# Hedgehog attention with layer norm and MLP: centring as a one-input operation, the layer norm weight moved into the PSUM copies and into w1

## The chip, the cores and the metric

The kernel runs on one core of a Trainium2 chip. The metric is the device time of one execution in microseconds. A core has a TensorE (PE, with weight loads as a second stream, PEld), a VectorE (DVE), a ScalarE (ACT), a GpSimd (POOL), and SyncE (SP), which issues most of the DMAs. All executions quoted here are fast ones by the label that each result carries. Where two kernels are compared, the ratio is the mean time of one kernel's fast runs over the mean of the other's fast runs of the same rounds, with a 95% interval. It is therefore not quite the ratio of the medians quoted beside it.

## The reference

Eight batches, eight heads, 576 positions, head size 64, 128 features. The attention's result is the input of a layer norm and a two-layer MLP with a residual.

```python
def _attn_ref(q, k, v, w_phi):
    def phi(x):
        proj = np.einsum('bhsd,df->bhsf', x, w_phi)
        proj = proj - np.max(np.abs(proj), axis=-1, keepdims=True)
        return np.concatenate([np.exp(proj), np.exp(-proj)], axis=-1)
    q_p, k_p = (phi(q), phi(k))
    kv = np.einsum('bhsf,bhsd->bhfd', k_p, v)
    z = np.sum(k_p, axis=2)
    num = np.einsum('bhsf,bhfd->bhsd', q_p, kv)
    den = np.einsum('bhsf,bhf->bhs', q_p, z)[..., None] + 1e-06
    return num / den

def _moe_ref(x, g_ln, w_ch1, w_ch2):          # x: 8 x 576 x 512
    mu = np.mean(x, axis=-1, keepdims=True)
    var = np.mean((x - mu) ** 2, axis=-1, keepdims=True)
    xn = (x - mu) / np.sqrt(var + 1e-06) * g_ln
    ch = np.maximum(xn @ w_ch1, 0.0) @ w_ch2  # 512 -> 2048 -> 512
    return x + ch
```

Dividing by the standard deviation commutes with the rectifier and with both products, so the kernel applies it at the very end. Only (x − mean)·g has to be ready ahead of the first product. The weight g belongs to a column of x, that is, to a row of w_ch1. So it can be multiplied into x, into the transposed x, or into w_ch1.

## The kernel before

The work goes in four pairs of batches. Each pair has nine tiles of 128 rows, taken in three rounds. For each tile, DVE makes the statistics, one engine centres (tile `xc`), the rows are transposed (`xT`; for pair 0 by the TensorE through PSUM, for the other pairs by a transposing DMA), and the products `hT_ps` (w1) and `ch_ps` (w2) follow. While the MLP of one pair runs, the attention of the next one is woven in between.

The order on each engine is not written by hand. Every operation is handed to a list scheduler with its inputs, its outputs and a **told duration for each engine that could do it**. `add_any` lets the scheduler choose the engine. Told durations steer the order; they are not what the chip takes. A change of one told number can therefore reorder everything behind it.

```python
            def center(e, i=i, t=t):
                ...
                if e == "DVE":
                    nc.vector.scalar_tensor_tensor(
                        out=xc, in0=x[:, t, :], scalar=pr["mv"][:, t, 0:1],
                        in1=gln_sb, op0=ALU.subtract, op1=ALU.mult,
                    )
                else:
                    xd = moe_sb.tile([P, DM], FP32, tag="xd", name="xd", bufs=1)
                    nc.gpsimd.tensor_tensor(
                        out=xd, in0=x[:, t, :], in1=bcast(pr["mv"][:, t, 0], 1, DM),
                        op=ALU.subtract,
                    )
                    nc.gpsimd.tensor_tensor(out=xc, in0=xd, in1=gln_sb, op=ALU.mult)
            ...
            add("DVE", 0.72, V, stats, ...)
            add_any({"DVE": 0.62, "POOL": 2.1}, V, center, ...)
...
            def copy(e, k0=k0, st=st):                      # pair 0 only: PSUM -> xT
                copy_on(
                    e, pr["xT", r][:, k0 : k0 + 2, 0:cols],
                    st["ps"][:, 0 : 2 * cols].rearrange("p (k n) -> p k n", k=2),
                )
            add_any({"DVE": 0.08 + 0.128 * n, "ACT": 0.12 + 0.21 * n}, V, copy, ...)
...
    dma("SP", 3.0, 262144, gln_sb, dram(moe_g_ln, 0, [[0, P], [1, DM]]), w=["gln"])
...
    FAST, SLOW, MOE_STEP = 4.9, 10.5, 0.92                  # spacing of the MLP's ranks
```

## Time and profile before

| | before |
|---|---|
| median of the three runs ahead of the prediction | 380.05 us (378.9 to 380.62) |
| profiled run: span, mean granted TensorE clock | 378.5 us, 0.982 |
| matmuls | 3348 |
| centrings | 19 on DVE, 17 on GpSimd (two operations each) |

The prediction below shows the page's busy shares and slices, windows of 10 us, a timeline and the groups. Two more windows of the kernel before are needed for the comparison. They come from the view that sums the busy time of each engine in a stretch; the columns are: stretch, length, then busy us and instruction count of PE, PEld, DVE, ACT, POOL, then the granted clock, the DMA share and GB/s.

```profile
80.00:100.00 20.00, 19.41 (x240) 12.30 (x239) 18.89 (x51) 17.85 (x49) 17.75 (x31) 1.00 0.86 182
120.00:140.00 20.00, 20.00 (x194) 11.65 (x193) 14.52 (x44) 11.32 (x28) 12.99 (x20) 1.00 0.73 185
```

The TensorE has next to no holes in either stretch. In the first, DVE has 1.1 us to spare in 20, in the second 5.5 us.

And from the view of waits of the TensorE, between 60 and 145 us (who waits for whom: total us, times, longest), all that it lists:

```profile
PE xT_ps L938 <- POOL xc L891: 0.5, 1, 0.5
PE pm L572 <- ACT ea L676: 0.3, 1, 0.3
PE kv L696 <- POOL vv L646: 0.2, 1, 0.2
```

### The profile page before, as it was taken

The page shows a single profiled execution, that of the slowest core. Times are in us where ns is not written, and L with a number is a line of the kernel's source. Part 1 is how long each engine was busy: PE and PEld are TensorE (multiplying, and loading weights), DVE is VectorE, ACT ScalarE, POOL GpSimd, SP SyncE. Part 2 cuts the span into 40 slices and gives each one's busy share as a digit, 9 for nine tenths or more (in the row PEclk, how much of TensorE's full clock was granted, in tenths as well). Part 3 has the DMA queues.
Part 4 walks back from the last instruction along what each step waited for, and adds up shares of the span by engine and source line. Part 5 has one row for each costly group of instructions (what it writes and reads, how often), then busy time and mean ns, then how long its engine had stood idle before and what let it go on. Part 6 is the DMA issues. An engine that isn't in the chain of part 4 may idle for free.

```text
span 378.5 us, 9097 instructions
## 1 busy us (share of the span) xinstructions
PE 351.5 (93%) x3348; PEld 207.8 (55%) x3348; DVE 275.4 (73%) x723; ACT 251.8 (67%) x640; POOL 207.3 (55%) x368
## 2 busy tenths in 40 slices
PE   3786589999999999999999999999999999999995
PEld 1464367556566555655556555555565545555553
DVE  3889989799879768977879999976767885000102
ACT  3999489799879638876689556977779306433310
POOL 5589669889857658864456647953546432000000
PEclk9999579999999999999999999999999999999999
DMA  6999999998949834488555743712200135110102
GB/s 177 282 264 228 174 281 258 272 165 142 280 138 238 237 100 99 83 182 226 172 134 141 223 99 78 174 29 58 58 28 29 50 88 102 28 57 28 55 32 83
DMA packets 88749, 52.70 MB, mean 139 GB/s; under 512 B 55040, under 2 KB 84096, under 8 KB 88704
## 3 DMA queue, kind: packets, MB, share of 16 engines
q1 hardware_dynamic: 83856, 47.37, 49.5%
q0 software_dynamic: 4224, 4.19, 6.8%
q10 hardware_dynamic: 624, 0.56, 0.5%
q8 instruction: 26, 0.43, 0.4%
q14 instruction: 19, 0.16, 0.2%
HBM read 37.03 MB, written 9.44 MB: 123 GB/s over the span
## 4 chain that ended last, share of the span: by engine, by line
PE 65%; ACT 5%; DVE 4%; POOL 2%; issue 1%; DVEq 0%; POOLq 0%; DMA 0%
PE ch_ps L1021 27%; PE hT_ps L989 27%; PE num L730 3%; PE kv L701 3%; ACT ea L676 2%; PE pm L572 2%; ACT EB L623 2%; DVE m L592 1%; PE pt L670 1%; DVE st L873 1%; ACT hT L999 1%; PE kv L696 1%; POOL xc L891 1%; POOL xd L887 1%; DVE xc L881 1%
## 5 line engine op out<-in xcount | busy, mean ns | idle before, releaser
L989 PE MATMUL hT_ps<-xT,w 128*128 128x384 bf16 x768 | 150.2, 327 | 1.0 <-ACT EB L623 0.7
L1021 PE MATMUL ch_ps<-w,hT 128*128 128x512 bf16 (+2 forms) x592 | 148.5, 373 | 0.0
L999 ACT ACTIVATE hT<-hT_ps 128x384 bf16<-128x384 f32 x130 | 63.9, 502 | 62.1 <-PE hT_ps L989 61.8
L989 PEld LDWEIGHTS <-w 128*128 128x128 bf16 x768 | 71.4, 98 | 54.4 <-issue 4.1
L592 DVE TENSOR_REDUCE m<-pm 128x4 f32<-128x512 f32 x128 | 82.1, 678 | 7.9 <-PE pm L572 7.5
L754 POOL TENSOR_TENSOR x<-numc,rden 128x192 bf16<-128x192 f32 (+1 forms) x112 | 50.5, 463 | 58.0 <-DVE rden L748 55.9
L1021 PEld LDWEIGHTS <-hT 128*128 128x128 bf16 x592 | 53.1, 98 | 45.8 <-issue 1.0
L676 ACT ACTIVATE ea<-pt 128x512 bf16<-128x512 f32 x128 | 67.7, 628 | 7.4 <-PE pt L670 7.4
L623 ACT ACTIVATE EB<-pm 128x512 bf16<-128x512 f32 x128 | 68.4, 628 | 4.8 <-DVE m L592 4.1
L1029 DVE SCALAR_TENSOR_TENSOR o<-ch_ps,rstd,x 128x512 f32<-128x512 f32 (+2 forms) x37 | 26.6, 726 | 54.1 <-PE ch_ps L1021 42.3
L637 POOL TENSOR_TENSOR vv<-v,emk 128x512 bf16<-128x512 f32 x32 | 33.5, 1047 | 36.8 <-ACT emk L608 23.2
L736 DVE TENSOR_TENSOR numc<-num,emq 128x195 f32<-128x195 f32 (+1 forms) x96 | 32.5, 344 | 20.2 <-PE num L730 15.5
L730 PEld LDWEIGHTS <-ea 128*128 128x128 bf16 x512 | 28.1, 100 | 15.5 <-issue 3.1
L997 DVE TENSOR_SCALAR hT<-hT_ps 128x384 bf16<-128x384 f32 x62 | 32.8, 539 | 2.1 <-PE hT_ps L989 1.8
L742 DVE TENSOR_TENSOR numc<-numc,num 128x195 f32<-128x195 f32 (+1 forms) x100 | 33.4, 342 | 0.7
L730 PE MATMUL num<-KV,ea 128*128 128x65 bf16 x512 | 31.9, 197 | 2.1 <-ACT EB L623 1.2
L637 POOL TENSOR_TENSOR vv<-v,en 128x512 bf16<-128x512 f32 x32 | 33.4, 1043 | 0.0
L873 DVE BATCH_NORM_STATS2 st<-x 128x6 f32<-128x512 bf16 x36 | 24.3, 674 | 4.1 <-POOL x L754 3.8
L701 PE MATMUL kv<-vv,EB 128*128 128x65 bf16 x512 | 25.4, 201 | 0.0
L572 PEld LDWEIGHTS <-qkT 64*128 64x128 bf16 x512 | 17.3, 100 | 13.6 <-issue 6.9
L887 POOL TENSOR_TENSOR xd<-x,mv 128x512 f32<-128x512 bf16 x17 | 18.8, 1105 | 9.9 <-DVE mv L874 8.8
L701 PEld LDWEIGHTS <-EB 128*128 128x128 bf16 x512 | 23.0, 102 | 2.0 <-issue 0.3
(67 smaller groups left out, 388.9 us busy)
## 6 DMA issues: line engine op xcount, KB each, us to landing
out_dram<-o SPq DMA_DIRECT2D x31, 256.0 KB, 2.3
qk<-in_k_dram SPq DMA_DIRECT2D x28, 256.0 KB, 5.0
v<-in_v_dram SPq DMA_DIRECT2D x28, 256.0 KB, 3.6
qk<-in_q_dram SPq DMA_DIRECT2D x26, 256.0 KB, 4.9
w<-in_moe_w_ch_dram POOLq DMA_DIRECT2D x8, 512.0 KB, 9.4
qk<-in_k_dram SPq DMA_DIRECT2D x2, 512.0 KB, 7.1
qk<-in_q_dram SPq DMA_DIRECT2D x2, 512.0 KB, 8.6
v<-in_v_dram SPq DMA_DIRECT2D x2, 512.0 KB, 10.2
```

Source lines behind the costliest of these rows:

```text
L592: nc.vector.reduce_max(out=u["m", i].rearrange("p (c e) -> p e c", e=2)[:, e], in_=u["pm", i, e], axis=AX.X, apply_absolute_value=True,)
L623: nc.scalar.activation(u["EB"][:, t, e * 4 : (e + 1) * 4].rearrange("p c f -> p (c f)"), u["pm", 1, e].rearrange("p c f -> p (c f)"), AF.E ...
L637: nc.gpsimd.tensor_tensor(out=u["vv"][:, t, 0:MX, 0:D], in0=vb[:, uu, :].rearrange("p (c d) -> p c d", d=D), in1=bcast(e[:, 0:MX], 2, D), ...
L676: nc.scalar.activation(u["EA"][:, t, e * 512 : (e + 1) * 512], u["pt", e], AF.Exp, scale=(1.0, -1.0)[t],)
L701: nc.tensor.matmul(ps[:, t, c // 4, :], EB[:, t, (c % 2) * 4 + c // 2, :], vv[:, t, c, :], start=False, stop=(t == 0 and c == MX - 1), ski ...
L730: nc.tensor.matmul(ps[:, t, i, :], lhsT, rhs, start=(j == 0), stop=(j == len(terms) - 1))
L742: nc.vector.tensor_add(out=st["numc"][:, 0:nch], in0=st["numc"][:, 0:nch], in1=st["ps"][:, 0])
L754: nc.gpsimd.tensor_tensor(out=dst, in0=st["numc"][:, i : i + cnt, 0:D], in1=bcast(st["rden"][:, i : i + cnt], 2, D), op=ALU.mult,)
L989: nc.tensor.matmul(st["ps"][:, 0:cols], w1_sb[:, kc, jj * P : (jj + 1) * P], pr["xT", r][:, kc, 0:cols], start=(kc == 0), stop=(kc == KC - 1),
L997: nc.vector.tensor_relu(h_sb[:, 0:cols], st["ps"][:, 0:cols])
L999: nc.scalar.activation(h_sb[:, 0:cols], st["ps"][:, 0:cols], AF.Relu)
L1021: nc.tensor.matmul(ch[t, c0], hT[r, jj][:, rt * P : (rt + 1) * P], w2_sb[:, jj, c0:c1], start=(jj == 0), stop=(jj == JC - 1),)
```

## The change

The centring becomes mean − x, with one tensor input, which ScalarE can do as well as DVE, and which GpSimd does in one operation instead of two. The sign goes into the weight: −g. For pair 0 the weight is the scale of the PSUM copies. After pair 0 it is multiplied into w1 in place, once, for pairs 1 to 3, whose rows never pass through PSUM on their way to `xT`. The weight's load shrinks from one row broadcast to all partitions (256 KB) to 2 KB. The intent is less work on DVE and GpSimd, the two engines that stood ahead of the first round of the MLP.

```diff
-    gln_sb = consts.tile([P, DM], FP32, name="gln")
+    gln_sb = consts.tile([P, KC], FP32, name="gln")
...
+    def scale_w1(n, rank):
+        def emit():
+            for kc in range(KC):
+                w = w1_sb[:, kc, n * WC : (n + 1) * WC]
+                nc.vector.tensor_scalar_mul(out=w, in0=w, scalar1=gln_sb[:, kc : kc + 1])
+        add("DVE", 0.9, rank, emit, r=["gln"], w=[("w1", n, kc) for kc in range(KC)])
...
-                if e == "DVE":
-                    nc.vector.scalar_tensor_tensor(
-                        out=xc, in0=x[:, t, :], scalar=pr["mv"][:, t, 0:1],
-                        in1=gln_sb, op0=ALU.subtract, op1=ALU.mult,
+                mean = pr["mv"][:, t, 0:1]
+                if e == "ACT":
+                    nc.scalar.activation(xc, x[:, t, :], AF.Identity, bias=mean, scale=-1.0)
+                elif e == "DVE":
+                    nc.vector.tensor_scalar(
+                        out=xc, in0=x[:, t, :], scalar1=-1.0, scalar2=mean,
+                        op0=ALU.mult, op1=ALU.add,
                     )
                 else:
-                    xd = moe_sb.tile([P, DM], FP32, tag="xd", name="xd", bufs=1)
                     nc.gpsimd.tensor_tensor(
-                        out=xd, in0=x[:, t, :], in1=bcast(pr["mv"][:, t, 0], 1, DM),
+                        out=xc, in0=bcast(pr["mv"][:, t, 0], 1, DM), in1=x[:, t, :],
                         op=ALU.subtract,
                     )
-                    nc.gpsimd.tensor_tensor(out=xc, in0=xd, in1=gln_sb, op=ALU.mult)
...
-            add_any({"DVE": 0.62, "POOL": 2.1}, V, center, ...)
+            add_any({"DVE": 0.35, "ACT": 0.5, "POOL": 1.05}, V, center, ...)
...
-                copy_on(
-                    e, pr["xT", r][:, k0 : k0 + 2, 0:cols],
-                    st["ps"][:, 0 : 2 * cols].rearrange("p (k n) -> p k n", k=2),
-                )
+                for kk in range(2):
+                    dst = pr["xT", r][:, k0 + kk, 0:cols]
+                    src, g_ = st["ps"][:, kk * cols : (kk + 1) * cols], gln_sb[:, k0 + kk : k0 + kk + 1]
+                    if e == "ACT":
+                        nc.scalar.activation(dst, src, AF.Copy, scale=g_)
+                    else:
+                        nc.vector.tensor_scalar_mul(out=dst, in0=src, scalar1=g_)
...
-            add_any({"DVE": 0.08 + 0.128 * n, "ACT": 0.12 + 0.21 * n}, V, copy, r=[key], ...)
+            add_any({"DVE": 0.14 + 0.14 * n, "ACT": 0.14 + 0.21 * n}, V, copy, r=[key, "gln"], ...)
...
-    dma("SP", 3.0, 262144, gln_sb, dram(moe_g_ln, 0, [[0, P], [1, DM]]), w=["gln"])
+    dma("SP", 3.0, 20000, gln_sb, moe_g_ln.rearrange("(kc p) -> p kc", p=P), w=["gln"])
+    add("DVE", 0.1, 3.0, lambda: nc.vector.tensor_scalar_mul(out=gln_sb, in0=gln_sb, scalar1=-1.0),
+        w=["gln"])
...
+                if w_["pair"] == 0:
+                    for i_ in range(NW):
+                        scale_w1(i_, moe_V)
```

More of the change, by code (lines that the diff above doesn't have):

```diff
@@ L896, in x_stats @@
             add("DVE", 0.72, V, stats, r=[("x", pair % NX, t, h) for h in range(H)], w=w)
-            add_any({"DVE": 0.62, "POOL": 2.1}, V, center, r=["gln"] + [("mv", pair % 2, t)] + [("x", pair % NX, t, h) for h in range(H)],
+            add_any({"DVE": 0.35, "ACT": 0.5, "POOL": 1.05}, V, center, r=[("mv", pair % 2, t)] + [("x", pair % NX, t, h) for h in range(H)],
                     w=[("xc", slot, i)])
@@ L956, in x_trans @@
                 w=[key, *wk], acquire=("B", 1))
-            add_any({"DVE": 0.08 + 0.128 * n, "ACT": 0.12 + 0.21 * n}, V, copy, r=[key], w=wk,
+            add_any({"DVE": 0.14 + 0.14 * n, "ACT": 0.14 + 0.21 * n}, V, copy, r=[key, "gln"], w=wk,
                     release=[("B", 1)])
```

## The prediction

> **What bounds the kernel now.** I read the page first: busy shares, then the slices.
>
> ```profile
> PE 351.5 (93%) x3348; PEld 207.8 (55%) x3348; DVE 275.4 (73%) x723; ACT 251.8 (67%) x640; POOL 207.3 (55%) x368
> ...
> PE   3786589999999999999999999999999999999995
> ...
> DVE  3889989799879768977879999976767885000102
> ACT  3999489799879638876689556977779306433310
> ...
> PEclk9999579999999999999999999999999999999999
> ```
>
> The TensorE is busy all the time except in the first six slices (a slice is 9.5 us) and at the end. The last six slices are nearly the TensorE alone: the second layer of the last rows, with nothing beside it that elementwise work could delay. So only the first 60 us and what small gaps remain in the middle can be won. I read those next from the windows of 10 us (busy us and instruction count of PE, PEld, DVE, ACT, POOL; granted clock; DMA share; GB/s).
>
> ```profile
> 30.00:40.00 10.00, 6.75 (x100) 4.50 (x96) 10.00 (x33) 9.22 (x26) 9.91 (x22) 0.89 1.22 210
> 40.00:50.00 10.00, 5.94 (x81) 5.05 (x79) 9.54 (x24) 4.75 (x13) 5.57 (x14) 0.50 0.96 169
> ...
> 130.00:140.00 10.00, 10.00 (x83) 5.57 (x82) 7.12 (x22) 2.75 (x9) 6.38 (x7) 1.00 0.54 157
> ...
> 330.00:340.00 10.00, 10.00 (x56) 5.29 (x54) 1.20 (x2) 3.62 (x8) 0.00 (x0) 1.00 0.14 54
> ```
>
> From 0 to 60 us the PE column adds up to 41.5 us, so 18.5 us idle; from 60 to 370 us all windows together lack only 4.1 us. Busy time flatters the PE, because ends are modelled, so I also laid the matmuls' start-to-start distances out. In the chain of work, four hT matmuls take 0.65 us and three ch matmuls 0.65 us, that is 0.1625 and 0.216 us each. 768 x 0.1625 = 124.8; 560 x 0.216 plus the split last tile = 124.8; attention, transposes and tails from their own spacings some 73.5. Sum 323.1 us. The span of 378.5 us thus holds about 55 us in which no matmul streams: 37 before 60 us (3.5 of it before the first matmul), 13.5 between 60 and 320, about 5 in the last result and store. These are the purse.
>
> The largest single hole is at 43 to 47 us, where the first round of layer-norm rows is prepared. Timeline (start, us, engine, line, op, count):
>
> ```profile
> 40.51 2.60 DVE L881 SCALAR_TENSOR_TENSOR xc<-x,mv,gln 128x512 bf16<-128x512 bf16 x1
> ...
> 41.04 1.03 POOL L637 TENSOR_TENSOR vv<-v,en 128x512 bf16<-128x512 f32 x1
> ...
> 44.65 1.38 DVE L881 SCALAR_TENSOR_TENSOR xc<-x,mv,gln 128x512 bf16<-128x512 bf16 x2
> ...
> 46.88 1.46 PE L938 MATMUL xT_ps<-ident,xc 128*128 128x128 bf16 x12 [3.76 <-DVE numc L742]
> ```
>
> PE idles 3.76 us. The wait names numc, but the row transposed is xc, and DVE carried the three statistics and three centrings from 39.5 to 46.0 us. One centring lasted 2.60 us instead of 0.72, while GpSimd was at work beside it.
>
> Last the groups, shapes kept apart (busy us, mean ns | idle before):
>
> ```profile
> L891 POOL TENSOR_TENSOR xc<-xd,gln 128x512 bf16<-128x512 f32 x17 | 22.7, 1334 | 1.3
> L881 DVE SCALAR_TENSOR_TENSOR xc<-x,mv,gln 128x512 bf16<-128x512 bf16 x19 | 20.7, 1109 | 0.0
> L887 POOL TENSOR_TENSOR xd<-x,mv 128x512 f32<-128x512 bf16 x17 | 18.8, 1105 | 9.9 <-DVE mv L874 8.8 <-DVE rden L748 0.8
> ```
>
> The 36 centrings cost 62 us of DVE and GpSimd together; DVE's mean of 1109 ns stands against a shortest of 719.
>
> **What the Trainium skill says.** *SBUF — State Buffer*, "SBUF: two separate sides": VectorE and GpSimd share a port pair as an exclusive lock, taken by a VectorE op with two SBUF inputs or in a two-port mode, for the whole instruction. The trace agrees: a centring started at 298.38 us beside a GpSimd op running 298.13 to 299.40 took 1571 ns, the next one 739. *VectorE: DVE Perf Modes*, "The perf-mode tier table": tensor_scalar from bf16 in SBUF reaches 4x, from PSUM at most 2x. The old trace has no such SBUF op; its PSUM copies of 512 and 768 columns (405 and 553 ns) agree with 2x: 0.58 ns a column. *ScalarE: Activation LUTs*, "What ACT_TABLE_LOAD costs": 186 ns + 0.833 ns a column, some 93 more for each pointer operand. The trace's 128x512 Exp took 628 ns against 613. *TensorE: Matmul & The Clock Gate*, "Back-to-back issue gap": N/2.4 + 2.5 ns, 162.5 for 384 columns: as measured above.
>
> **The change part by part.** The build's instruction order gives the counts.
> - Centring. Before: 19 on DVE (21.1 us by count times mean), 17 on GpSimd in two ops (41.5 us). After: 3 on DVE, 19 on ScalarE, 14 on GpSimd in one op. DVE at 4x: 512/4/0.96 + 139 ns fixed (539 ns of a 384-column relu less 400) = 0.27 us, 0.8 in all. ScalarE: 628 + 93 = 0.72, 13.7 in all. GpSimd 14 x 1.04 (the old xd's median) = 14.6.
> - PSUM copies of pair 0 with the weight as scale. Six copies of 768 columns (DVE 3 x 0.553, ACT 3 x 0.798) become 12 of 384: DVE 8 x 0.33, ACT 4 x 0.60 = 2.6 and 2.4 us. DVE +1.0, ACT 0.
> - Scaling w1 in place after pair 0: 16 DVE ops of 128x512 bf16, 16 x 0.27 = 4.3 us, plus lock waits: perhaps 1 us for each of the four batches of four. They stand far enough behind pair 0's last product and ahead of pair 1's first one; no matmul should wait long.
> - The scheduler answers: 11 relus go from ACT to DVE (+5.9 us DVE, -5.5 ACT), about one 1024-column cast comes from ACT to each of DVE and GpSimd (+1.0 each, -2.1).
> - The weight's load falls from 256 KB to 2 KB of 4-byte pieces, with one tiny negation. Roughly neutral: fewer bytes, slower issue.
> Sums: DVE -21.1 + 0.8 + 1.0 + 4.3 + 5.9 + 1.0 = -8, or -4 with lock waits; ACT +13.7 - 5.5 - 2.1 = +6; GpSimd -41.5 + 14.6 + 1.0 = -26. PE does the same 3348 matmuls.
>
> On the path: in the first round DVE's block shrinks from 6.5 to about 2.9 us (three statistics of 0.86, one centring of 0.27), but two of the centrings now stand in GpSimd's queue behind two vv blocks, and end around 44.6 us; transposes start some 2.2 us earlier. Four DVE copies in a row (1.3 us) where ACT and DVE worked side by side (about 1.1) give little back. With ACT and DVE no longer clogged there I book 3 us in the front. Between 60 and 320 us the relief of GpSimd and DVE meets only 13.5 us of gaps; I book 2 us, less 0.5 for scaling w1. Total 4.5: 380.05 - 4.5 = 375.5 us.
>
> **Rivals.**
> 1. Nothing comes out (379 to 381). For: PE is full from 60 us; GpSimd, which gains most, is not the bound; ScalarE, at 9.2 of 10 in the front, gets two centrings of pair 0. Against: the hole at 43 us really is the centring, and ACT lay idle for half of 40 to 50 us.
> 2. A larger gain (below 372). The half clock from about 38 to 51.5 us lies over the hole; were the PE kept busy there, the throttle might not fall and some 3 us more come, and every later gap could shrink. For: the granted clock is 0.50 there. Against: it fell at 37.9, before the hole, from idling earlier, which the change does not touch; it may also just move.
> 3. Slower (382 and more). The negation of the weight stands early in DVE's queue, about 20 us in; if the 512 small pieces land late, DVE stalls. Or w1 scaling waits on the lock and delays relus. For: small loads landed 6 to 7 us after issue, giving about 19 us, close. Against: each is worth 1 or 2 us at most.
>
> **Range and chances.** Predicted 375.5 us, a gain of 1.2%. A reshuffled order alone may shift 2 us either way, rival 1 lies at +4.5, rival 2 at -5: range 370.5 to 380.0. Faster by 2% means below 372.4: 0.18. Within 2%: 0.78. Slower: 0.04.
>
> **What would show it.** Right: PE's sum of matmul work unchanged; first hT matmul at about 48 us instead of 50.1; the gap before xT transposes 1 to 2 us; DVE centring near 0.27 us when alone and ACT's near 0.72; GpSimd busy near 181 us; from 320 us on the same tail. Wrong: if the first hT moves but the end does not, later gaps ate it; if the end moves by more than 7 us, look at the clock and at the gaps from 60 to 320. A DVE wait on the weight's load near 20 us would show rival 3.

## The result, and the profile after

The changed kernel took **377.35 us** (median of 4 runs, 376.75 to 377.95), the kernel before 380.03 us (4 runs). The ratio of the fast runs is **0.9933 [0.9904, 0.9963]**: a gain of 0.7%, inside the predicted range, smaller than the 1.2% predicted. Measured again in a later session it was 0.9915 [0.9889, 0.9941]. The profiled run has a span of 375.2 us, 3.3 us less than before, at a mean clock of 0.983 (before 0.982).

The page of the changed kernel, busy shares and slices (40 slices, tenths):

```profile
PE 349.1 (93%) x3306; PEld 208.0 (55%) x3348; DVE 273.1 (73%) x738; ACT 257.5 (69%) x650; POOL 182.4 (49%) x349
...
PE   2888789989999899999999999999999999999995
...
DVE  3889989979879999987879979978788672000102
ACT  3889698799879648876569768966589437433310
...
PEclk9998799999999999999999999999999999999998
```

The record lacks 42 matmuls (3306 of 3348); the weight loads are complete, and I count by those. GpSimd lost 25 us of busy time, DVE only 2.3, ScalarE gained 5.7. In the first six slices the TensorE has more, and the half clock is milder. But slices 9 and 14 (75 to 84 and 122 to 131 us) now fall below nine tenths, where the page before had nines throughout.

The windows that answer to those shown of before:

```profile
30.00:40.00 10.00, 7.69 (x97) 5.43 (x96) 9.32 (x31) 9.24 (x27) 9.15 (x20) 0.83 1.17 189
40.00:50.00 10.00, 8.90 (x103) 6.38 (x105) 8.50 (x29) 6.87 (x24) 8.22 (x17) 0.66 0.63 131
...
80.00:100.00 20.00, 18.50 (x215) 11.51 (x216) 16.85 (x47) 17.59 (x49) 15.62 (x29) 1.00 1.22 225
120.00:140.00 20.00, 18.77 (x179) 11.04 (x180) 19.51 (x58) 12.16 (x28) 9.22 (x19) 1.00 0.63 179
```

From 40 to 50 us there are 105 weight loads instead of 79. From 80 to 100 there are 216 instead of 239, and from 120 to 140 it is 180 instead of 193, with DVE at 19.5 of 20 us where it had been at 14.5.

The timeline of the first round of layer-norm rows, which holds the old hole of 3.76 us (start, us, engine, line, op, count):

```profile
39.64 2.04 POOL L897 TENSOR_TENSOR xc<-mv,x 128x512 bf16<-128x512 f32 x2
...
41.32 0.50 DVE L892 TENSOR_SCALAR xc<-x,mv 128x512 bf16<-128x512 bf16 x1
...
42.49 1.44 PE L947 MATMUL xT_ps<-ident,xc 128*128 128x128 bf16 x12 [0.60 <-ACT ea L684]
...
43.54 1.38 DVE L963 TENSOR_SCALAR xT<-xT_ps,gln 128x384 bf16<-128x384 bf16 x4
...
45.51 0.82 PE L1001 MATMUL hT_ps<-xT,w 128*128 128x384 bf16 x2
```

The hole ahead of the transposes is 0.60 us instead of 3.76, and the first hT matmul comes at 45.5 us instead of 50.1. The groups, shapes kept apart, and the spread of the w1 scaling (ns: least, median, most):

```profile
L897 POOL TENSOR_TENSOR xc<-mv,x 128x512 bf16<-128x512 f32 x14 | 14.5, 1038 | 10.3 <-DVE mv L882 3.9 <-issue 2.5 <-ACT xc L890 2.0
L890 ACT ACTIVATE xc<-x,mv 128x512 bf16<-128x512 bf16 x19 | 13.8, 725 | 14.6 <-DVE mv L882 12.2 <-DVE rden L756 2.2
L892 DVE TENSOR_SCALAR xc<-x,mv 128x512 bf16<-128x512 bf16 x3 | 1.5, 510 | 0.0
...
L963 DVE TENSOR_SCALAR xT<-xT_ps,gln 128x384 bf16<-128x384 bf16 x8 | 2.8, 402 | 0.0
...
L398 DVE TENSOR_SCALAR w<-w,gln x16: 315/342/1128, 110.9 to 136.9; 128x512 bf16<-128x512 bf16 x16
```

**A ledger of the TensorE.** To see where the time came from and went, I gave each weight load the streaming time of its matmul and summed these over time. For the streaming time of N columns I take N/2.4 + 2.5 ns, which the Trainium skill, *TensorE: Matmul & The Clock Gate*, "Back-to-back issue gap", gives for the gap of one matmul by itself. The traces show it from start to start in full streams as well, for 384 columns (162.5 ns) and 512 (216 ns; for a sustained stream of 512 that section has about 131 ns, which these traces do not show). Matmuls of 64 rows count half, since eight of them end 0.40 us after the first one starts while one alone takes 0.21. That is an estimate, but its total, 320.7 us by the counts, lies within 1% of the 323.1 of the prediction. The table gives how far each profile is ahead of the kernel before, in us of matmul work done by that time. Each row is one profiled run, so differences of half a microsecond mean little, and larger ones can be chance too: the changed kernel has two rows that differ by up to 0.5 us, the one without scaling two that differ by up to 1.2. A profiled run is also not always a typical one: those of e1, e6, e8 and e10 are the slowest of their kernels, that of e9 the fastest.

| ahead of before at (us) | 60 | 80 | 100 | 120 | 140 | 220 | 260 | 320 |
|---|---|---|---|---|---|---|---|---|
| changed kernel | +3.3 | +2.4 | +1.0 | +0.7 | −0.2 | +0.5 | +3.4 | +3.2 |
| changed kernel, second session | +2.8 | +2.1 | +0.8 | +0.5 | −0.5 | +0.2 | +3.0 | +2.9 |
| e1, no w1 scaling | +3.7 | +2.1 | +0.2 | +0.2 | −0.1 | +1.1 | +3.7 | +3.6 |
| e10, the same again | +3.3 | +1.0 | −0.5 | −1.0 | −1.0 | 0.0 | +2.7 | +2.4 |
| e9, w1 scaled twice | +4.4 | +2.9 | +1.0 | −0.8 | −3.6 | −5.0 | −2.1 | −2.4 |
| e7, scaling on ScalarE | +3.9 | +3.4 | +1.9 | +1.9 | +1.1 | +1.9 | +4.3 | +4.5 |
| e2, order kept, short centring | +0.5 | +1.2 | +1.6 | +1.6 | +1.5 | +2.2 | +3.6 | +3.6 |
| e3, order kept, DVE's part | +0.8 | +1.0 | +1.4 | +1.4 | +1.3 | +2.1 | +2.8 | +2.9 |
| e6, whole change, order kept | +0.2 | +1.0 | +0.4 | 0.0 | −0.9 | −2.4 | −1.3 | −1.5 |
| e8, before, other order | 0.0 | −1.6 | −2.8 | −3.3 | −3.7 | −3.4 | −3.2 | −5.8 |

So the changed kernel won 3.3 us in the front, as booked, **lost all of it between 60 and 140 us**, and won 3 us again between 220 and 260, in the first rounds of pair 2. Since 3.3 − 2.3 − 1.2 + 0.7 + 2.9 − 0.2 = 3.2, the sum of these stretches is close to the 3.3 us between the two spans. The experiments ask what took the lead back, and what the parts of the change are worth.

### The profile page after: what moved, and what is told of

Its sections match the earlier page's. It is cut to its first block, busy times and chain, and to the rows that moved or that the text cites. A ratio compares the mean times of both kernels' runs of the same rounds, so it can differ in the third digit from the quotient of the medians.

```text
span 375.2 us, 9069 instructions
## 1 busy us (share of the span) xinstructions
PE 349.1 (93%) x3306; PEld 208.0 (55%) x3348; DVE 273.1 (73%) x738; ACT 257.5 (69%) x650; POOL 182.4 (49%) x349
## 4 chain that ended last, share of the span: by engine, by line
PE 74%; DVE 9%; DMA 6%; ACT 6%; issue 2%; POOL 2%; SPq 0%; DVEq 0%; POOLq 0%
PE ch_ps L1033 30%; PE hT_ps L1001 29%; DMA qkT<-qkb 4%; PE num L738 4%; PE kv L709 4%; PE pm L580 3%; ACT EB L631 3%; DVE m L600 3%; DMA qk<-in_k_dram 2%; ACT ea L684 1%; PE pt L678 1%; DVE numc L744 1%; DVE numc L750 1%; PE kv L704 1%; DVE st L881 1%
## 5 line engine op out<-in xcount | busy, mean ns | idle before, releaser
L1033 PE MATMUL ch_ps<-w,hT 128*128 128x512 bf16 (+2 forms) x550 | 141.0, 373 | 2.7 <-issue 0.9
L1011 ACT ACTIVATE hT<-hT_ps 128x384 bf16<-128x384 f32 x119 | 58.5, 496 | 58.9 <-PE hT_ps L1001 58.4
L684 ACT ACTIVATE ea<-pt 128x512 bf16<-128x512 f32 x128 | 69.0, 637 | 7.2 <-PE pt L678 7.1
L1009 DVE TENSOR_SCALAR hT<-hT_ps 128x384 bf16<-128x384 f32 x73 | 39.0, 542 | 4.9 <-PE hT_ps L1001 4.3
L890 ACT ACTIVATE xc<-x,mv 128x512 bf16<-128x512 bf16 x19 | 13.8, 725 | 14.6 <-DVE mv L882 12.2
```

Source lines behind the costliest of these rows:

```text
L684: nc.scalar.activation(u["EA"][:, t, e * 512 : (e + 1) * 512], u["pt", e], AF.Exp, scale=(1.0, -1.0)[t],)
L1009: nc.vector.tensor_relu(h_sb[:, 0:cols], st["ps"][:, 0:cols])
L1011: nc.scalar.activation(h_sb[:, 0:cols], st["ps"][:, 0:cols], AF.Relu)
L1033: nc.tensor.matmul(ch[t, c0], hT[r, jj][:, rt * P : (rt + 1) * P], w2_sb[:, jj, c0:c1], start=(jj == 0), stop=(jj == JC - 1),)
```

## The experiments

Twelve kernels ran in three sessions, each with five rounds; in each session the kernel before ran alongside (medians 380.72, 380.80 and 380.48 us). The expectations, quoted as they stood before each run, speak of theories. Theory A: attention, which produces the rows, sets the pace after 60 us whatever the order, so a lead is waited away. Theory B: the w1 scaling on DVE costs what is missing. Theory D: the scheduler was told wrong durations, and the true ones give a better order. Further rivals are described in the texts themselves.

### 1. Leave the scaling out

```diff
                 w = w1_sb[:, kc, n * WC : (n + 1) * WC]
-                nc.vector.tensor_scalar_mul(out=w, in0=w, scalar1=gln_sb[:, kc : kc + 1])
+                pass
```

The order stays that of the changed kernel; the result is wrong on purpose (pairs 1 to 3 lack the weight). It ran in the first session and again in the third.

> The changed kernel in its own instruction order, with the 16 DVE instructions that scale w1 left out (the result is wrong on purpose: pairs 1 to 3 lack weight and sign). The changed kernel measured 377.35 us. Theory A (the lead of 3.3 us that PE had at 60 us was lost by 140 us because the attention work on ScalarE and VectorE sets the pace there, whatever the scaling): less than 0.7 us changes, 376.6 to 377.6. Theory B (the 6.7 us of scaling on a full VectorE took it): 1 to 2 us come back, 375.3 to 376.3, and the matmul work done by 140 us is at least 1 us ahead of the changed kernel's.

> The run without scaling once more, next to the doubled one: 0.9855 to 0.9885 if theory B holds, 0.991 to 0.994 if not.

Measured: 376.47 us, ratio **0.9869 [0.9848, 0.9889]**, and in the third session 376.92 us, **0.9903 [0.9874, 0.9933]**. The changed kernel itself was run again in the second session:

> The changed kernel once more, on the chip of its neighbours in this call, so that the other runs can be set against it and not against a measurement of another hour. Every theory: ratio to the kernel before 0.990 to 0.996, that is 376.5 to 378.7 us. If it comes out below 0.989, the 0.9869 of the run without scaling was a matter of the chip and theory B (scaling costs 1 to 2 us) falls.

Measured: 377.56 us, **0.9915 [0.9889, 0.9941]**.

The first session put the scaling at 0.6% (0.9933 against 0.9869), the later ones at 0.1% (0.9915 against 0.9903), with intervals that overlap. The cost of the scaling is thus of the order of 1 us (the mean of 0.6 and 0.1% is 1.4 us) and not well separated from zero by these times alone. The expectations were set to tell theory A from theory B, and they did not: 376.47 us lies between their two ranges, 0.9903 between the two of the second run, and the lead at 140 us that theory B asked for did not appear (−0.1 against −0.2). The trace shows one place where it costs. This is the timeline of the changed kernel around the second hole:

```profile
122.65 2.37 DVE L398 TENSOR_SCALAR w<-w,gln 128x512 bf16<-128x512 bf16 x4
...
123.12 1.09 POOL L645 TENSOR_TENSOR vv<-v,en 128x512 bf16<-128x512 f32 x1
...
124.95 1.27 DVE L600 TENSOR_REDUCE m<-pm 128x4 f32<-128x512 f32 x2
...
125.68 0.81 PE L1001 MATMUL hT_ps<-xT,w 128*128 128x384 bf16 x4 [0.97 <-DVE m L600]
```

Four scalings took 2.37 us where four at the median of 342 ns would take 1.37; a GpSimd multiplication ran across them. The reductions queued behind them came late, and the TensorE stood for 0.97 us. In both runs without scaling this hole is gone. The ledger says the same: from 100 to 140 us the changed kernel loses 1.2 and 1.3 us, without scaling 0.3 and 0.5. So the scaling takes **about 0.9 us in that stretch**. That it takes 0.9 of the 3.5 us lost between 60 and 140 is not shown: without it e1 and e10 lost 3.8 and 4.3 there, since they lost more before 100 us, when no scaling has started (the first is at 110.9 us). A lead is lost with the scaling and without it.

### 2. Double the scaling

```diff
                 nc.vector.tensor_scalar_mul(out=w, in0=w, scalar1=gln_sb[:, kc : kc + 1])
+                nc.vector.tensor_scalar_mul(out=w, in0=w, scalar1=gln_sb[:, kc : kc + 1])
```

Wrong on purpose as well.

> The changed kernel in its own order with each of the 16 scalings of w1 done twice (wrong on purpose: the weight is squared for pairs 1 to 3). The run without scaling was at 0.9869 of the kernel before, the changed kernel at 0.9933 and 0.9915. Theory B (scaling on VectorE costs some 1.8 us of the end): 0.996 to 1.000. If scaling is hidden and the 0.9869 was a matter of the chip: as the changed kernel, 0.991 to 0.994.

Measured: 383.59 us, **1.0089 [1.0057, 1.0122]**. The 16 added operations were busy for 6.5 us, and the time rose by 1.6 to 1.7% over the two measurements with one dose (0.9933 and 0.9915), 5.9 to 6.6 us: the second dose went to the end nearly in full, the first by a fraction. Both expectations were too low. The windows fit a slack that the first dose used up: between 120 and 140 us DVE has 3.6 to 3.8 us to spare in the same order without scaling (e10, e1), 0.5 with one dose and 0.6 with two (the kernel before, in its own order, had 5.5). In the ledger the doubled kernel falls from +1.0 at 100 us to −5.5 at 160. A second reading fits as well and no run separates the two: the longer the block, the later whatever is queued behind it. The four blocks of scaling lasted 1.4 to 2.4 us in the changed kernel and 2.8 to 4.1 here, and behind the first one (110.95 to 114.1 us) the TensorE stood 1.40 us for a DVE operation of the attention, where the changed kernel shows no such hole. Theory B holds in that work on DVE in that stretch can turn into time, but the single dose that the change carries costs little of it.

### 3. What was lost between 60 and 100 us

No kernel was run for this stretch alone; the evidence is in the profiles of all the runs. The timeline of the changed kernel around its largest hole there:

```profile
81.93 0.86 DVE L291 CAST qkb<-qk 128x1024 bf16<-128x1024 f32 x1 [1.92 <-issue]
...
82.71 1.01 DVE L1009 TENSOR_SCALAR hT<-hT_ps 128x384 bf16<-128x384 f32 x2
...
83.31 0.96 PE L947 MATMUL xT_ps<-ident,xc 128*128 128x128 bf16 x12 [0.91 <-DVE hT L1009]
```

DVE stood idle for 1.92 us ahead of a cast of the next q and k to bf16, with two rectifiers queued behind it. The transposes that needed the PSUM buffers of these rectifiers stood for 0.91 us. The profile names no releaser here ("issue"), but two other runs of nearly the same order do. The view of waits of DVE, first in the second session's run of the changed kernel:

```profile
DVE qkb L291 <- DMA qk<-in_q_dram: 1.4, 1, 1.4
```

then in e7 (the scaling on ScalarE):

```profile
DVE qkb L291 <- DMA qkT<-qkb: 2.0, 1, 2.0
```

and the TensorE's own waits in e10, which has no scaling at all:

```profile
PE pm L580 <- DMA qkT<-qkb: 1.7, 1, 1.7
PE xT_ps L947 <- DVE hT L1009: 0.9, 1, 0.9
```

The casts feed a transposing DMA (qkT from qkb), and they can't start before q and k have landed and the previous transpose has let go of its buffer. The landing times of the DMAs say what ended this wait: in all six profiles of the changed order this cast, which comes between 80.7 and 83.5 us, starts 0.07 to 0.08 us after a qkT transpose landed (at 81.85 us in the changed kernel). The corresponding cast in the kernel before, and the issue of the corresponding transpose, first before and then after:

```profile
81.81 0.76 DVE L291 CAST qkb<-qk 128x1024 bf16<-128x1024 f32 x1
...
74.19 1.24 SPq L524 DMA_TRANSPOSE qkT<-qkb  x1
...
75.10 2.26 SPq L532 DMA_TRANSPOSE qkT<-qkb  x1
```

Before, the transpose issued at 74.19 us landed at 77.96, and the cast did not wait. After, the two casts ahead of it ran 1.3 us earlier, but it was issued 0.9 us later and landed 3.9 us later. So the cast comes at 81.9 us in both kernels, and what was won ahead of it is gone. In all six profiles of the changed order (the changed kernel twice, e1, e7, e9, e10), and in e4 and e12 with other orders, DVE idles 1.4 to 3.9 us ahead of such casts between 60 and 110 us. In the kernel before, e2, e3, e6 and e8, none of which had a lead of over 1 us at 60, it does not. The one other profile with a lead, e11 (+4.0 at 60), shows 0.9 us, behind GpSimd, and kept the most of its lead up to 100 us: +2.6. But by 140 us it too is down to +0.4, without such a wait. The DMA share between 80 and 100 us is 1.22 after and 0.86 before, and the slowest landing of a qkT transpose between 60 and 110 us, the first one, took 10.3 us after and 6.9 before (10.4 in e11). The reading is that **the front's lead ran into the transfers**: the kernel reaches the first of these casts about 3 us earlier (59.2 against 62.2 us), the transposes do not land earlier, and an engine that works in a fixed order waits with everything queued behind the cast. The profiles show which wait ended last, but no run took these transfers away, so it is argued and not proven that the lead would have lasted without them. It is theory A in a narrower form. As I had stated it, "whatever the order", it is not what happens: e2 and e3 kept a lead of 1.3 to 1.9 us from 100 to 140 us with the old order. One rival stays untested: a ceiling on the lead that attention sets. No profile is more than 1.5 us ahead at 140 us, whether it stood at +0.5 (e2) or +4.0 (e11) at 60 us.

### 4. The old order with a short centring

```diff
-                    nc.vector.scalar_tensor_tensor(
-                        out=xc, in0=x[:, t, :], scalar=pr["mv"][:, t, 0:1],
-                        in1=gln_sb, op0=ALU.subtract, op1=ALU.mult,
+                    nc.vector.tensor_scalar(
+                        out=xc, in0=x[:, t, :], scalar1=pr["mv"][:, t, 0:1], scalar2=None,
+                        op0=ALU.subtract,
...
-                        out=xd, in0=x[:, t, :], in1=bcast(pr["mv"][:, t, 0], 1, DM),
+                        out=xc, in0=x[:, t, :], in1=bcast(pr["mv"][:, t, 0], 1, DM),
...
-                    nc.gpsimd.tensor_tensor(out=xc, in0=xd, in1=gln_sb, op=ALU.mult)
```

This is the kernel before with the weight left out of the centring on both engines (e2), or on DVE alone (e3: the first hunk). Told durations are untouched, so the order is exactly that of before. Results are wrong on purpose.

> The kernel before in its own instruction order and engine choice, with every centring cut to one subtraction on VectorE and GpSimd, and the weight left out (wrong on purpose). Theory A (shorter centring on VectorE fills the hole at 43 us): the first hT matmul moves from 50.0 to about 47 us and the time falls to 376 to 378. Rival C (the gain came from the new order and from ScalarE taking the centring): 379.3 to 380.5.

> As the run before, but only VectorE's 19 centrings are cut; GpSimd keeps its two instructions per centring. Theory A says the hole at 43 us was VectorE's alone: the same front as the run before, and a time within 0.7 us of it. If GpSimd's double work mattered (through the shared port or as a late centring at the pair boundaries), this one is slower by 1 us or more than the run before, and its VectorE centrings are still stretched when GpSimd is at work.

Measured: e2 377.35 us, **0.9903 [0.9885, 0.992]**; e3 378.03 us, **0.9922 [0.9902, 0.9941]**. With the order fixed, short centring is worth 3.7 us (0.97% of 380.7), and DVE's share alone 3.0 us. GpSimd's share adds 0.7 us by the difference, within the intervals. This is what the removed work is worth by itself, and it is no less than what the whole change gained with its own order. The times came out as theory A of these two runs had it, but not by its mechanism: the first hT matmul moved to 49.8 us in e2 and 49.2 in e3 (50.1 before, about 47 expected), the hole ahead of the transposes is still 2.3 and 2.6 us, and the ledger puts only 0.5 and 0.8 us in the front. Of the 3.6 and 2.9 us won by 320 us, most is won after 60 us, where the prediction had booked 2.

The first round suggests why the front needed the new order. The timeline of e2:

```profile
41.64 1.81 DVE L881 TENSOR_SCALAR xc<-x,mv 128x512 bf16<-128x512 bf16 x1
41.76 1.04 POOL L637 TENSOR_TENSOR vv<-v,en 128x512 bf16<-128x512 f32 x1
...
46.42 1.24 PE L936 MATMUL xT_ps<-ident,xc 128*128 128x128 bf16 x12 [2.25 <-DVE numc L742]
```

and the spread of all its DVE centrings (ns: least, median, most):

```profile
L881 DVE TENSOR_SCALAR xc<-x,mv x19: 321/348/1808, 41.6 to 310.3; 128x512 bf16<-128x512 bf16 x19
```

An operation of 321 ns took 1808, while GpSimd was at work beside it. *SBUF — State Buffer*, "SBUF: two separate sides", in the Trainium skill says that a DVE operation in a two-port mode locks the shared port pair just as one with two SBUF inputs does; here that costs some 1.5 us. Taking the second input away did not take the lock away. In the changed kernel's order two of the three centrings went to GpSimd itself, ahead of its next block, and DVE's took 0.50 us.

### 5. The whole change with the order kept

```diff
-            add_any({"DVE": 0.35, "ACT": 0.5, "POOL": 1.05}, V, center, ...)
+            add_any({"DVE": 0.62, "POOL": 2.1}, V, center, ...)
...
-            add_any({"DVE": 0.14 + 0.14 * n, "ACT": 0.14 + 0.21 * n}, V, copy, ...)
+            add_any({"DVE": 0.08 + 0.128 * n, "ACT": 0.12 + 0.21 * n}, V, copy, ...)
```

The changed kernel's operations with the durations told before. The order on the TensorE is then 96% that of before (the changed kernel's own: 77%); ScalarE centres nothing. The result is correct.

> The whole change, correct, but the scheduler told the old durations for centring (0.62 us on VectorE, 2.1 on GpSimd, no ScalarE) and for the copies, so that the order and the engine choice stay close to the kernel before's. Theory E (the change's own order loses 2 us between 77 and 135 us that the old order doesn't): 375.5 to 377, faster than the changed kernel by about 1 us, PE's matmul work at 140 us at least 1 us ahead of the changed kernel's, first hT matmul near 49.5. Theory A (attention's pace limits whatever the order): within 0.7 us of the changed kernel.

Measured: 380.64 us (22 runs), **0.999 [0.9978, 1.0003]**. That is 0.9% more than e2. Both expectations missed: theory E's by 3.6 us, and theory A's (within 0.7 us of the changed kernel) by about 2.4. The front came as expected, the first hT matmul at 49.6 us. It differs from e2 by the weight: the split copies and the 16 scalings (7.1 us on DVE here, mean 502 ns, against 6.7 and 477), and by the few per cent of order that these bring about. In the ledger e6 falls behind e2 by 0.3 us up to 60 us, by 1.2 to 100, by 2.4 to 140 and by 4.6 to 220. Scaling stands between 111 and 137 us, so it can be charged with at most the third of these steps directly. Part of the gap is chance: the profile of e6 is of its slowest run (381.64 us), that of e2 of its fastest (376.72). The loss after 140 us comes when no instruction of the change but the centring is left, and I have no run that explains it. It stays open.

### 6. Measured durations for the scheduler

```diff
-        add("DVE", 0.9, rank, emit, r=["gln"], ...)
+        add("DVE", 1.6, rank, emit, r=["gln"], ...)
...
-            add_any({"DVE": 0.35, "ACT": 0.5, "POOL": 1.05}, V, center, ...)
+            add_any({"DVE": 0.50, "ACT": 0.73, "POOL": 1.05}, V, center, ...)
...
-            add_any({"DVE": 0.14 + 0.14 * n, "ACT": 0.14 + 0.21 * n}, V, copy, ...)
+            add_any({"DVE": 0.20 + 0.20 * n, "ACT": 0.18 + 0.32 * n}, V, copy, ...)
```

> The changed kernel with the scheduler told the measured durations: centring 0.50 us on VectorE, 0.73 on ScalarE, 1.05 on GpSimd; PSUM copies 0.80 and 1.14 us for two blocks of 384; scaling 1.6 us for four. Theory D (the loss between 60 and 140 us comes from an order built on durations that are too short: ScalarE's centring was put down as 0.50 and took 0.725): 375 to 376.5. Theory A: within 0.8 us of 377.35, as the order only shuffles.

Measured: 378.97 us (18 runs), **0.9954 [0.9937, 0.9971]**; correct. Telling the truth about the new operations made the kernel no faster than the changed one; if anything slower. The same picture shows in its ledger: +3.8 at 60 us, +0.6 at 120, and at 320 only +1.3. Both expectations missed (theory A's by 0.8 us). Theory D gets no support, but the order on the TensorE is only 76% that of the changed kernel, and by section 8 a new order alone can move more than this, so one order is not enough to drop it.

### 7. The scaling on ScalarE

```diff
-                nc.vector.tensor_scalar_mul(out=w, in0=w, scalar1=gln_sb[:, kc : kc + 1])
+                nc.scalar.activation(w, w, AF.Copy, scale=gln_sb[:, kc : kc + 1])
...
-        add("DVE", 0.9, rank, emit, r=["gln"], ...)
+        add("ACT", 2.9, rank, emit, r=["gln"], ...)
```

ScalarE had 7.8 us to spare between 120 and 140 us.

> The changed kernel with the 16 scalings of w1 on ScalarE (about 0.72 us each, 11.5 us in all) instead of VectorE (6.7 us). The scheduler orders anew. Theory B2 (scaling hurt because VectorE waited for the port that GpSimd held): the scalings last 0.72 us each with no stretch, and 0.5 to 1 us is won over the changed kernel. Theory F (what hurts is work on a full engine in that stretch, and ScalarE is as full): no better than the changed kernel, or up to 1 us slower.

Measured: 377.02 us, **0.9896 [0.9866, 0.9925]**; correct. One scaling takes 709 to 807 ns there, 10.4 us in all. It is the best correct version by its ratio, and of the correct ones in the table it kept the largest lead, +1.1 at 140 us and +4.5 at 320. But its interval overlaps with that of the changed kernel in the same session (0.9915), so I don't call it faster, and it decides nothing between theories B2 and F. On top of it I forbade centring on ScalarE:

```diff
-            add_any({"DVE": 0.35, "ACT": 0.5, "POOL": 1.05}, V, center, ...)
+            add_any({"DVE": 0.50, "POOL": 1.05}, V, center, ...)
```

> The change with centring on VectorE and GpSimd alone and the scaling of w1 on ScalarE: a candidate that takes 19 x 0.725 us off ScalarE and 16 scalings off VectorE. Theory F (what counts is what the full engines carry between 60 and 140 us): 0.985 to 0.989, better than both kernels. If the shuffle of the order decides: 0.987 to 1.002.

Measured: 382.44 us (13 runs), **1.0037 [1.0012, 1.0063]**; correct, and slower than before. Its profile has a TensorE hole of 3.2 us at 87 us, behind a qkT transpose, that no other one has, and DVE idles 3.7 us ahead of one cast there. Both expectations missed. The candidate was lost; and since the order changed as well, it does not prove that centring belongs on ScalarE.

### 8. What order alone is worth

The last two runs change one number that has nothing to do with the change: the spacing of the MLP's ranks, in the kernel before (e8) and in the changed one (e11).

```diff
-    FAST, SLOW, MOE_STEP = 4.9, 10.5, 0.92
+    FAST, SLOW, MOE_STEP = 4.9, 10.5, 0.90
```

> The kernel before with one pacing constant of the scheduler at 0.90 in place of 0.92: the same instructions in another order (a little over half of VectorE's sequence stays), nothing else. It measures what a new order alone does. Theory A and E both leave this open; if it moves by more than 1.5 us (below 378.5 or above 382 against some 380.5), then differences of 1 us between kernels with different orders prove nothing about the change, and only the runs that keep an order do.

> The changed kernel with the pacing constant at 0.90 in place of 0.92, the partner of the reordered kernel before, which ran at 1.0114. If the change is worth 0.7 to 0.9% in any order, this one comes to 1.002 to 1.006. If its worth hangs on the order, anything from 0.985 to 1.015.

Measured: e8 385.27 us, **1.0114 [1.009, 1.0137]**; e11 376.78 us, **0.9904 [0.9878, 0.993]**; both correct. The same instructions in another order (64% alike on the TensorE) cost 1.1%, and of the two expectations for e11 the second held: what the change is worth hangs on the order. In that second order the change is worth 2.1% (0.9904/1.0114 = 0.979), in the first 0.7 to 0.9%. In the changed kernel the same new number, which leaves 52% of the TensorE's order alike, moves the time by only 0.1 to 0.3% (0.9904 against 0.9915 and 0.9933), so the 1.1% is one case and not a measure for every kernel. A verdict of "this part gives 0.5%" between two kernels whose orders differ can thus be below the noise of reordering. Among my runs those with the same order are before/e2/e3, and the changed kernel/e1/e5/e9/e10; e7 is 97% like the changed kernel and e6 96% like the kernel before. I rest on these.

## Why the prediction was right or wrong

The time, 377.35 us, lay in the range, and the class "within 2%" was right. The predicted 375.5 was 1.85 us too low. Step by step:

- **The front, booked at 3 us: right.** The ledger has +3.3 at 60 us (2.8 in the second session). The hole ahead of the transposes shrank to 0.60 us, more than the 1 to 2 foreseen, and the first hT matmul came 4.6 us earlier, not 2.1. The four scaled copies on DVE took 1.38 us against 1.3 booked. That the sum came out at 3 is partly luck: the two centrings on GpSimd ended at 41.7 us and not around 44.6, so the transposes started 4.4 us earlier and not 2.2, and the half clock, which the sum left out, was shorter (see rival 2).
- **Durations on ScalarE and GpSimd: right.** Centring on ScalarE 725 ns (0.72), on GpSimd 1038 (1.04), GpSimd busy 182.4 us (181), ScalarE +5.7 us (+6).
- **Durations on DVE: too low.** Centring was put at 0.27 us; in the changed kernel it took 0.35 to 0.68, and 0.32 was the least in any run, so the fixed part, taken over from a rectifier that reads PSUM (139 ns), was about 50 ns short. The scaling was put at 0.27 each plus about 1 us of lock wait per batch of four, 8.3 in all at worst; it took 6.7, from 0.315 to 1.128 each, so the stretching was there, but smaller. The scaled copies took 402 ns against 330. DVE's relief was −2.3 us against −4 to −8.
- **The middle, "2 us, less 0.5 for scaling w1": the net is the term that failed.** Between 60 and 320 us the ledger shows no gain at all (+3.3 at 60, +3.2 at 320), where +1.5 was booked. The gain existed, and was even larger: +2.9 between 220 and 260 us, where pair 2's first rounds are centred. What was missing in the sum is the loss: 2.3 us between 60 and 100, which I had not booked at all, since I read the small gaps there as an upper limit to gains and not as a sign that a lead can't be kept; and 1.2 us between 100 and 140, where the runs without scaling lose 0.3 to 0.5 (0.5 was booked for scaling in all). The first of these, in every profile of that order, goes with waits for the transfers of q and k; that they are its cause is argued.
- **Rivals.** Rival 1 (nothing comes out) was half right: the front's gain did come and was given back, but for another reason than "GpSimd is not the bound". Rival 2: the half clock did become shorter (10.2 us at half speed in two stretches, before 13.65 in one), and it began at 31.7 us instead of 37.9. It may be part of the 3.3 in front: e9, which has the same instructions up to 111 us, had 6.8 us of half clock and was at +4.4 at 60 us, the other four profiles of that order had 10.2 and +2.8 to +3.7. But no run separates it, and no further gain came. Rival 3 did not happen: the weight landed 4.9 us after its issue at 12.0 us (before: 6.7), the issue itself was no slower (468 ns against 465), and the negation ran at 19.7 without a wait. Its second half, scaling delaying what stands behind it, did happen once, at 125.7 us, for 0.97 us.
- **"A reshuffled order alone may shift 2 us either way": too small.** e8 shows 4.5 us for one.

## What to carry to other kernels

When a schedule is static, a lead won early is kept only if nothing later arrives by its own clock: look for the next transfer that an in-order engine has to wait for, before booking the gain at the end. Price a part of a change with the instruction order held fixed, and measure once what a reordering with no change of work does; here that was 1.1%, more than the whole change gained. And a first dose of work on a busy engine that is not the bound says little about a second: here the first dose of scaling cost about 1 us of 6.7, the second some 6 of 6.5. Look at the slack of that stretch, and at how long one block holds up the queue behind it.

## What the Trainium skill lacked or had wrong

- *VectorE: DVE Perf Modes*, "The perf-mode tier table": it has no row for scalar_tensor_tensor. With 512 bf16 columns from SBUF it took 719 ns at the least here; tensor_scalar with one input took 315 to 322.
- The same page does not say whether a per-partition scalar makes an operation from PSUM longer. The scaled copy of 384 bf16 columns took 402 ns, about as long as the plain copy of 512 (405 ns), so the estimate from the plain copies (330) was 70 ns short.
- *SBUF — State Buffer*, "SBUF: two separate sides": the traces agree, and with more effect than I expected for one-input operations: 321 ns alone, 1808 ns beside GpSimd in e2, and the w1 scaling from 315 to 1128 ns. The page gives no figure for such a wait of a DVE operation; in e2 it spanned three GpSimd operations in a row (41.76 to 43.29 us), and the page does not say which engine comes next when one of them ends.
- *ScalarE: Activation LUTs*, "What ACT_TABLE_LOAD costs": its formula with one pointer operand, 186 + 0.833·512 + 93 = 706 ns, an estimate by that page, was within 3% of the 725 ns measured for the centring. Nothing to mend.
- No page tells what the order of instructions alone is worth in a kernel with five busy engines: 1.1% here for one unrelated number of the scheduler.
